# Decoding four weight blocks beside the last two pairs of k, zero passes at the head, and a later transpose

## The chip, the cores and the metric

The kernel runs on one core of a Trainium2 chip. The metric is the device time of one execution in microseconds (us), here the median of three runs. The engines have short names in what follows: PE (TensorE, with PEld for its weight loads), DVE (VectorE), ACT (ScalarE), POOL (GpSimd) and SP (SyncE, which issues the DMAs here).

## The reference, cut to what matters

Linear attention with random features on `q`, `k` and `v` (2 batches, 8 heads, 576 tokens, 64 wide, 128 features), then a feed-forward layer with `h - tanh(h)`, then a sum over four experts with ReLU. The change touches the first two.

```python
def phi(x):
    proj = np.einsum('bhsd,md->bhsm', x, omega)
    h = proj - np.sum(x * x, axis=-1, keepdims=True) / 2.0
    return np.exp(h - np.max(h, axis=-1, keepdims=True)) / np.sqrt(m)
kv = np.einsum('bhsm,bhsd->bhmd', phi(k_s), v)
z = np.sum(phi(k_s), axis=2)
out = einsum(phi(q_s), kv) / (einsum(phi(q_s), z) + 1e-6)
...
h = x @ w_in          # 1152x512 by 512x2048
g = h - np.tanh(h)
y = g @ w_out
```

`w_in` and `w_out` arrive as 64-bit floats and are turned into fp32 on the chip.

## The kernel before, in words

Every product in the part at hand is made of three passes of PE on operands split into a high and a low half (`th` and `tl`, `hh` and `hl`, `wah` and `wal`): high by high, high by low, low by high.

**The k stage** (up to about 43 us). The eight heads go as four pairs `p`. A pair's tokens are nine blocks of 128 rows in five groups (`kgroups`): four groups of two blocks from `kn`, and one of the last 64 tokens of each batch from `kr`, which holds all pairs. `features` (L296) gives two lists of generators. `transposed` (L304) turns four blocks at a time on PE (L299), copies the high half (`th`, ACT L304, or DVE L302 for the second four) and makes the low half (`tl`, DVE L306). `projected` (L318) makes six matmuls into `psP` (L317; three for the last group), the negated row maxima `nm` on DVE (L320), and four exponentials `kf` on ACT (L325; two for the last group). There are two `psP` banks. The products of a pair with v (`k_products`, `psV`, L337) run beside the next pair's groups, as `post`. The loop that begins at `for p in range(NP)` writes the order of PE, DVE and ACT by hand; POOL and SP follow a scheduler. Its `turn` says which transposes stand beside which group: those of the pair's own `kr` beside its second group (`i == 1`), the next pair's beside its fourth and fifth.

**Decoding a block** (class `Decoded`). 128x512 64-bit words are loaded into `raw`, of which there are four buffers. `scaled` makes `y` on ACT (L115). `joins` makes `m` on DVE: a shift (`top`, L128, or on ACT as `topped`, L121), a join with `y` and a join with `raw` (both L131), called here shift, y and raw. `parted` splits `m`: high half on ACT (L71), low half on POOL (L72). Before the change blocks 0 and 1 of the first four of w_in (`first[0]`, `first[1]`) are decoded beside the third and the fourth pair, one step a group; blocks 2 and 3, and the four of w_out, are decoded in the q loop (`LATER`).

**The q loop** (`for u in range(1, NU + 3)`, then `for e in ...`) is ordered by a scheduler. Twelve units of q go through projection, transposes (`psQ`, `qt`), attention (`psN`, L371 and L374, divided on DVE, L376 to L378) and the way back (`psX`, `x`, L385 and L72). Behind them `early` computes the first four columns of blocks of the feed-forward layer, in twelve units of 512, 384 and 256 tokens: `pse` (L485) in a PSUM bank, then `minus_tanh`, whose steps are named by letters: on ACT u (L495), q (L496), t (L497), m (L498), h (L503), on DVE a (L499), b (L500), s (L501), c (L502), and l on POOL (L504). Step s overwrites `pse` with `pse - t`, and c copies that into `y` where a mask says so, so the bank is held until c.

**Behind it** (from `po`, L598, at 125 us) the feed-forward layer runs in an order written by hand, then the experts. Lines of the profile are those of the kernel before.

Of the kernel before, what the change touches and what calls it, by code (L numbers as in the profile page):

```python
# [26 lines left out]
def tile_favor_attention__then__two_moe(  # L27
# [231 lines left out]
    load_v(1)  # L259
    ob = [ac.tile([P, 2 * P], F32R, name=f"ob{a}") for a in range(2)]  # L260
# [151 lines left out]
    LATER = {j - 1: (load_a, wa, 0, j) for j in range(2, NJ)} | {3 + j: (load_b, wb, 0, j) for j in range(NJ)}  # L412
# [3 lines left out]
    def k_pair(p):  # L416
        rest = kr[:, 2 * p:2 * p + 2, :].rearrange("p h d -> p (h d)")
        kT[p], kR[p] = features(lambda b, h: kn[p][:, b, h], rest, kgroups, lambda: kf[p], kp, k=True)

    first = {}  # L420
    with tc.manual_schedule(engines={mybir.EngineType.DVE, mybir.EngineType.PE, mybir.EngineType.Activation}):
        transposed_omega()
        k_pair(0)
        for i in range(2):
            whole(kT[0][i])
        post = []
        for p in range(NP):
            w = [first[p - 2].scaled, *first[p - 2].joins()] if p > 1 else []
            kf[p] = kp.tile([P, NT, 2, M], F32, tag="xf", name="kf")
            for i in range(len(kgroups)):  # L430
                if i == 3 and p + 1 < NP:
                    k_pair(p + 1)
                turn = kT[p][2:] if i == 1 else kT[p + 1][i - 3:i - 2] if i > 2 and p + 1 < NP else []
                run(lambda x=x: next(x) for x in turn)
                R = kR[p][i]
                next(R)
                next(R)
                run(lambda x=x: next(x) for x in turn)
                next(R)
                run(post[i:i + 1])  # L440
                run(w[i:i + 1])
                if i == 1 and p + 2 < NP:
                    kn.append(load_k(p + 2))
                    first[p] = load_a(0, p)
            if p > 1:
                wa[0, p - 2] = first[p - 2].parted()
# [44 lines left out]
    def minus_tanh(ps, hh, hl, t, u, y, view, eng_lo):  # L491

        vec, act = nc.vector, nc.scalar
        return dict(
# [6 lines left out]
            s=lambda: vec.tensor_tensor(out=ps, in0=ps, in1=view(t), op=ALU.subtract),  # L501
            c=lambda: vec.copy_predicated(view(y), view(u).bitcast(I32), ps),  # L502
# [24 lines left out]
    def early(e):  # L527
# [10 lines left out]
        g = minus_tanh(ps, gs[0, j][0][:, s], gs[0, j][1][:, s], t, u, y, lambda z: z, nc.gpsimd)  # L538
# [439 lines left out]
```

## Time and profile before

| | |
|---|---|
| median of three runs | 682.95 us (681.95 to 683.59) |
| the profiled execution | 683.97 us, of which 681.8 is the span |
| busy share of the span | PE 97%, DVE 78%, ACT 47%, POOL 10% |
| chain that ended last | PE 77%, DVE 13%, ACT 6% |
| recorded clock of PE | 1.000 |

The span counts from the first instruction to the last; the 2.2 us around it belong to every run. A row of a timeline gives start and duration in us, engine, line, operation, output and inputs, and in brackets how long its engine stood idle before and what ended that. Starts of neighbours on one engine can be closer than the duration, since operations overlap at their ends. The end of a matmul is modelled, so a busy PE may hide short pauses.

### The profile page before, as it was taken

To read this page: it belongs to the slowest core of one execution; us is meant where nothing else is said; L and a number is where in the kernel's file an instruction comes from. 1 tells how busy PE (TensorE), PEld (TensorE's weight loads), DVE (VectorE), ACT (ScalarE), POOL (GpSimd) and SP (SyncE) were. 2 spreads that over 40 slices of the span, in tenths; PEclk is the share of its full clock that TensorE was granted. 3 is DMA by queue.
4 is the path that set the end of the run, shared out by engine and by line. 5 is a ranking of instruction groups with operands and counts; after the bars stand their busy time and mean duration, and the time that the engine had idled before them with its cause. 6 is when DMAs were issued, how large, how long until landed. Compare 5 with 4: busy or idle time off the path is not lost.

```text
span 681.8 us, 10488 instructions
## 1 busy us (share of the span) xinstructions
PE 664.7 (97%) x4219; PEld 615.2 (90%) x4219; DVE 532.9 (78%) x832; ACT 317.1 (47%) x589; POOL 67.5 (10%) x66
## 2 busy tenths in 40 slices
PE   5999999899999999999999999999999999999997
PEld 4879889899999999998899999999988999999996
DVE  4788789799999987969387777777776777777664
ACT  4789998767767757435122223222232223232120
POOL 2032113522222210100000000000000000000000
PEclk9999999999999999999999999999999999999999
DMA  7953110212222222012001011111212020120004
GB/s 200 290 181 93 63 32 4 91 62 75 90 84 82 87 50 92 31 38 56 1 31 62 32 32 62 42 51 32 62 32 62 32 62 32 32 62 1 1 1 139
DMA packets 42768, 43.75 MB, mean 64 GB/s; under 512 B 5600, under 2 KB 37600, under 8 KB 42720
## 3 DMA queue, kind: packets, MB, share of 16 engines
q1 hardware_dynamic: 42720, 43.08, 21.1%
q8 instruction: 33, 0.54, 0.3%
q14 instruction: 15, 0.12, 0.1%
HBM read 40.72 MB, written 2.36 MB: 63 GB/s over the span
## 4 chain that ended last, share of the span: by engine, by line
PE 77%; DVE 13%; ACT 6%; issue 2%; DMA 1%; SPq 0%; POOL 0%; DVEq 0%
PE po L719 29%; PE Y L702 23%; PE po L598 7%; PE psh L485 7%; PE psP L317 3%; DVE m L131 3%; PE pse L485 2%; DVE y L499 2%; PE psN L371 2%; DVE y L502 1%; DVE y L500 1%; ACT y L496 1%; PE psQ L360 1%; ACT m L121 1%; DVE psh L501 1%
## 5 line engine op out<-in xcount | busy, mean ns | idle before, releaser
L725 DVE SCALAR_TENSOR_TENSOR oacc<-po,pr,oacc 128x512 f32<-128x512 f32 (+1 forms) x136 | 101.4, 746 | 34.2 <-PE po L719 33.8
L719 PE MATMUL po<-wbh,hl 128*128 128x512 f32 x290 | 112.9, 389 | 0.4 <-DVE hl L522 0.4
L719 PE MATMUL po<-wbh,hh 128*128 128x512 f32 x290 | 112.9, 389 | 0.1
L719 PE MATMUL po<-wbl,hh 128*128 128x512 f32 x290 | 112.9, 389 | 0.0
L719 PEld LDWEIGHTS po<-wbh,hl 128*128 128x128 f32 x290 | 54.4, 188 | 12.3 <-DVE hl L522 0.8
L719 PEld LDWEIGHTS po<-wbh,hh 128*128 128x128 f32 x290 | 54.7, 188 | 8.2 <-DVE oacc L725 0.3
L598 PE MATMUL po<-hh,wbh 128*128 128x384 f32 x180 | 60.8, 338 | 0.7 <-DVE y L502 0.5
L719 PEld LDWEIGHTS po<-wbl,hh 128*128 128x128 f32 x290 | 54.4, 188 | 7.5
L890 ACT ACTIVATE hh<-Y 128x576 fp32r<-128x576 f32 x42 | 27.4, 653 | 72.5 <-DVE Y L887 64.0
L598 PE MATMUL po<-hl,wbh 128*128 128x384 f32 x180 | 60.7, 337 | 0.2
L598 PE MATMUL po<-hh,wbl 128*128 128x384 f32 x180 | 60.4, 336 | 0.0
L702 PE MATMUL Y<-y,wah 128*128 128x288 f32 x336 | 57.9, 294 | 0.0
L485 PE MATMUL psh<-x,wah 128*128 128x384 f32 x288 | 57.9, 336 | 0.0
L702 PEld LDWEIGHTS Y<-y,wah 128*128 128x128 f32 x336 | 51.2, 188 | 3.6 <-DVE hl L522 0.3
L485 PEld LDWEIGHTS psh<-x,wah 128*128 128x128 f32 x288 | 50.5, 188 | 0.0
L702 PE MATMUL Y<-Th,wal 128*128 128x288 f32 x224 | 47.8, 295 | 0.0
L702 PE MATMUL Y<-Tl,wah 128*128 128x288 f32 x224 | 47.6, 294 | 0.0
L702 PE MATMUL Y<-Th,wah 128*128 128x288 f32 x224 | 47.6, 293 | 0.0
L890 ACT ACTIVATE hh<-u 128x576 fp32r<-128x576 f32 x14 | 9.6, 687 | 73.5 <-DVE u L887 73.5
L702 PEld LDWEIGHTS Y<-Th,wah 128*128 128x128 f32 x224 | 39.0, 188 | 4.5
L503 ACT ACTIVATE hh<-y 128x1152 fp32r<-128x1152 f32 (+3 forms) x26 | 20.7, 798 | 41.7 <-DVE y L502 41.7
L672 ACT ACTIVATE wah<-y 128x512 fp32r<-128x512 f32 x28 | 17.6, 631 | 41.1 <-DVE y L652 41.1
(140 smaller groups left out, 1464.5 us busy)
## 6 DMA issues: line engine op xcount, KB each, us to landing
raw<-in_moe_w_dram SPq DMA_DIRECT2D x30, 512.0 KB, 3.6
raw<-in_moe_w_in_dram SPq DMA_DIRECT2D x16, 512.0 KB, 3.6
raw<-in_moe_w_out_dram SPq DMA_DIRECT2D x16, 512.0 KB, 3.4
kn<-in_k_dram SPq DMA_DIRECT2D x8, 256.0 KB, 4.4
vn<-in_v_dram SPq DMA_DIRECT2D x8, 256.0 KB, 5.6
qn<-in_q_dram SPq DMA_DIRECT2D x8, 256.0 KB, 5.4
out_dram<-oacc SPq DMA_DIRECT2D x7, 256.0 KB, 2.2
raw<-in_moe_w_dram SPq DMA_DIRECT2D x4, 256.0 KB, 2.9
```

The source lines that it names most:

```text
L131: vec.scalar_tensor_tensor(out=self.m, in0=x, scalar=scalar, in1=self.m, op0=op, op1=ALU.bitwise_or)
L317: nc.tensor.matmul(ps[:, i].rearrange("p a m -> p (a m)"), x[:, c], o, start=j == 0, stop=j == 2)
L371: nc.tensor.matmul(ps[:, j, h, :VC], qt[g][:, j, h, :], kvz[p][:, t // (TB + 1), h, :], start=True, stop=True)
L485: nc.tensor.matmul(ph[i, j][:, n, :CH] if bank is None else bank, w[:, c], x[:, n * CH:(n + 1) * CH] if bank is None else x[:, n], start=z ...
L499: a=lambda: vec.scalar_tensor_tensor(out=y, in0=y, scalar=CB, in1=u, op0=ALU.add, op1=ALU.mult),
L503: h=lambda: act.activation(hh, y, AF.Copy),
L598: nc.tensor.matmul(po[:, :CH], w[:, r], g[:, s], start=j == 0 and z == 0, stop=j == NJ - 1 and z == 2,)
L672: nc.scalar.activation(w[0], src, AF.Copy)
L702: nc.tensor.matmul(ps[:, m, :HN // 2], w[:, kk], b[:, m * HN // 2:(m + 1) * HN // 2], start=first and kk == 0 and z == 0, stop=kk == 1 and ...
L719: nc.tensor.matmul(po, g[:, s], w[:, cols], start=j == 0 and z == 0, stop=j == 1 and z == 2)
L725: nc.vector.scalar_tensor_tensor(out=acc, in0=po, scalar=pr[:, t, e:e + 1], in1=acc, op0=ALU.mult, op1=ALU.add)
L890: nc.scalar.activation(halves(gs[NA + q, f][0][:, h * HN:(h + 1) * HN]), x, AF.Relu)
```

## The change

Four things. Before the k stage PE makes matmuls over a tile of zeros into a spare `psN` bank: six ahead of the transpose of omega, six behind it, two between the first two sets of four transposes. For the first pair, the transpose of its `kr` tokens moves from the second group to the fourth, and that of the next pair's first half from the fourth to the third. Blocks 0 and 1 of w_in are decoded beside the third pair, 2 and 3 beside the fourth, the second of each two one group behind the first; the blocks of w_out move up by one unit of the q loop. And in `early` step s writes its difference to `t` in SBUF, and c reads it there.

```diff
+    zero = kp.tile([P, 2 * P], F32R, name="zero", bufs=1)
+    nc.vector.memset(zero.bitcast(F32), 0.0)
+    idle = ps_n.tile([P, 512], F32, tag="n", name="idle")
+    def busy(n):
+        for _ in range(n):
+            nc.tensor.matmul(idle[:, :2 * P], zero[:, :P], zero, start=True, stop=True)
...
-    LATER = {j - 1: (load_a, wa, 0, j) for j in range(2, NJ)} | {3 + j: (load_b, wb, 0, j) for j in range(NJ)}
+    LATER = {2 + j: (load_b, wb, 0, j) for j in range(NJ)}
...
+    def turns(p, i):
+        if i == 1 + 2 * (p == 0):
+            return kT[p][2:]
+        if p + 1 < NP and i in ((2, 4) if p == 0 else (3, 4)):
+            return kT[p + 1][i == 4:1 + (i == 4)]
+        return []
...
+        busy(6)
         transposed_omega()
+        busy(6)
         k_pair(0)
         for i in range(2):
             whole(kT[0][i])
+            if i == 0:
+                busy(2)
         post = []
         for p in range(NP):
-            w = [first[p - 2].scaled, *first[p - 2].joins()] if p > 1 else []
+            w = [[first[j].scaled, *first[j].joins()] for j in range(2 * p - 4, 2 * p - 2)] if p > 1 else []
             kf[p] = kp.tile([P, NT, 2, M], F32, tag="xf", name="kf")
             for i in range(len(kgroups)):
-                if i == 3 and p + 1 < NP:
+                if i == 2 and p + 1 < NP:
                     k_pair(p + 1)
-                turn = kT[p][2:] if i == 1 else kT[p + 1][i - 3:i - 2] if i > 2 and p + 1 < NP else []
+                turn = turns(p, i)
...
-                run(w[i:i + 1])
+                for z, x in enumerate(w):
+                    if i >= z:
+                        run(x[i - z:i - z + 1])
                 if i == 1 and p + 2 < NP:
                     kn.append(load_k(p + 2))
-                    first[p] = load_a(0, p)
+                if i == 1 and p < 3 or (p, i) == (1, 3):
+                    first[len(first)] = load_a(0, len(first))
             if p > 1:
-                wa[0, p - 2] = first[p - 2].parted()
+                for j in range(2 * p - 4, 2 * p - 2):
+                    wa[0, j] = first[j].parted()
...
+        d = view(t) if free else ps
...
-            s=lambda: vec.tensor_tensor(out=ps, in0=ps, in1=view(t), op=ALU.subtract),
-            c=lambda: vec.copy_predicated(view(y), view(u).bitcast(I32), ps),
+            s=lambda: vec.tensor_tensor(out=d, in0=ps, in1=view(t), op=ALU.subtract),
+            c=lambda: vec.copy_predicated(view(y), view(u).bitcast(I32), d),
...
-        g = minus_tanh(ps, gs[0, j][0][:, s], gs[0, j][1][:, s], t, u, y, lambda z: z, nc.gpsimd)
+        g = minus_tanh(ps, gs[0, j][0][:, s], gs[0, j][1][:, s], t, u, y, lambda z: z, nc.gpsimd, free=True)
```

How the order of instructions moves, at three places. Lines of the changed kernel are 9 to 27 higher. The first is ACT in the first pair of k, from the first `th`; before:

```order
L304 ACTIVATE th_153<-psT_155 128x512
L325 ACTIVATE kf_169<-psP_170,nm_177 128x128 x4
L304 ACTIVATE th_153<-psT_183 128x128
L325 ACTIVATE kf_169<-psP_186,nm_193 128x128 x4
L325 ACTIVATE kf_169<-psP_205,nm_212 128x128 x4
L304 ACTIVATE th_218<-psT_220 128x512
L325 ACTIVATE kf_169<-psP_226,nm_233 128x128 x4
L325 ACTIVATE kf_169<-psP_246,nm_250 128x128 x2
```

and now:

```order
L313 ACTIVATE th_168<-psT_170 128x512
L334 ACTIVATE kf_186<-psP_187,nm_194 128x128 x4
L334 ACTIVATE kf_186<-psP_200,nm_207 128x128 x4
L313 ACTIVATE th_218<-psT_220 128x512
L334 ACTIVATE kf_186<-psP_226,nm_233 128x128 x4
L313 ACTIVATE th_168<-psT_240 128x128
L334 ACTIVATE kf_186<-psP_243,nm_250 128x128 x4
L334 ACTIVATE kf_186<-psP_263,nm_267 128x128 x2
```

The `th` of the `kr` tokens (128x128) stood behind the first four exponentials and stands behind the third four; the next pair's first `th` (tile `th_218`) is now ahead of it.

The second is DVE from the last `kvz` copy inside the fourth pair to the residuals `tl` of q; before:

```order
L342 COPY kvz2_141<-psV_543 128x260
L131 SCALAR_TENSOR_TENSOR m_597<-raw_310,m_597 128x512
L320 TENSOR_REDUCE nm_652<-psP_648 128x2
L131 SCALAR_TENSOR_TENSOR m_825<-y_823,m_825 128x512
L128 TENSOR_SCALAR m_906<-raw_902 128x512
L131 SCALAR_TENSOR_TENSOR m_825<-raw_821,m_825 128x512
L131 SCALAR_TENSOR_TENSOR m_906<-y_904,m_906 128x512
L306 TENSOR_TENSOR tl_663<-psT_665,th_662 128x512
```

and now (`sm` and `pr` are the sums over the experts' shares, which stood at the end of the q loop):

```order
L351 COPY kvz2_144<-psV_574 128x260
L131 SCALAR_TENSOR_TENSOR m_628<-raw_393,m_628 128x512
L131 SCALAR_TENSOR_TENSOR m_656<-y_630,m_656 128x512
L329 TENSOR_REDUCE nm_688<-psP_684 128x2
L131 SCALAR_TENSOR_TENSOR m_656<-raw_479,m_656 128x512
L128 TENSOR_SCALAR m_935<-raw_931 128x512
L598 TENSOR_REDUCE sm_1922<-pr_72 128x9
L131 SCALAR_TENSOR_TENSOR m_935<-y_933,m_935 128x512
L599 TENSOR_SCALAR sm_1922<-sm_1922 128x9
L131 SCALAR_TENSOR_TENSOR m_935<-raw_931,m_935 128x512
L128 TENSOR_SCALAR m_1022<-raw_1018 128x512
L315 TENSOR_TENSOR tl_704<-psT_706,th_703 128x512
```

Behind the last maximum of k (128x2) there were a y, a shift, a raw and a y join ahead of `tl`; now there are three joins, two shifts and two operations on `sm`, and between the copy and that maximum one join more.

The third is DVE at the end of the q loop, from a raw join that both have there; before:

```order
L131 SCALAR_TENSOR_TENSOR m<-raw,m 128x512
L500 SCALAR_TENSOR_TENSOR y<-y,pse 128x384
L501 TENSOR_TENSOR pse<-pse,t 128x384
L572 TENSOR_SCALAR sm<-sm 128x9
L131 SCALAR_TENSOR_TENSOR m<-y,m 128x512
L502 COPY_PREDICATED y<-u,pse 128x384
L499 SCALAR_TENSOR_TENSOR y<-y,u 128x256
L573 RECIPROCAL sm<-sm 128x9
L500 SCALAR_TENSOR_TENSOR y<-y,pse 128x256
L501 TENSOR_TENSOR pse<-pse,t 128x256
L574 TENSOR_TENSOR pr<-pr,sm 128x36
L131 SCALAR_TENSOR_TENSOR m<-raw,m 128x512
```

and now:

```order
L131 SCALAR_TENSOR_TENSOR m<-raw,m 128x512
L527 SCALAR_TENSOR_TENSOR y<-y,pse 128x384
L528 TENSOR_TENSOR t<-pse,t 128x384
L72 TENSOR_TENSOR x_806<-psX,x_805 128x256
L529 COPY_PREDICATED y<-u,t 128x384
L526 SCALAR_TENSOR_TENSOR y<-y,u 128x384
L527 SCALAR_TENSOR_TENSOR y<-y,pse 128x384
L528 TENSOR_TENSOR t<-pse,t 128x384
L529 COPY_PREDICATED y<-u,t 128x384
```

A y and a raw join and the operations on `sm` and `pr` are gone from between the steps of `early`; steps s and c, now L528 and L529, name `t` in place of `pse`.

## Rows read from the trace of the kernel before

**Rows 1.** Stretches: us, then PE, PEld, DVE, ACT, POOL busy; clock, DMA share, GB/s.

```profile
35.10:43.00 7.90, 7.27 (x119) 6.38 (x118) 6.11 (x13) 7.36 (x25) 1.87 (x2) 1.00 0.49 146
...
50.00:103.00 53.00, 52.65 (x411) 47.76 (x410) 45.40 (x117) 48.97 (x128) 10.25 (x8) 1.00 0.20 63
103.00:125.20 22.20, 19.66 (x134) 18.41 (x132) 21.21 (x49) 19.44 (x49) 10.97 (x9) 1.00 0.13 41
```

**Rows 2.** Timeline of PE, end of q loop: start, us, operation, [idle <-releaser].

```profile
116.39 0.39 PE L485 MATMUL pse<-x,wah 128*128 128x256 f32 x1 [0.71 <-DVE x L72]
...
123.03 0.51 PE L485 MATMUL pse<-x,wah 128*128 128x256 f32 x2 [1.36 <-DVE y L502]
...
125.17 0.44 PE L598 MATMUL po<-hh,wbh 128*128 128x384 f32 x1 [0.47 <-DVE y L502]
```

**Rows 3.** Timeline of the head, PE and ACT.

```profile
4.47 1.12 PE L299 MATMUL psT<-ident,kn 128*128 128x128 f32 x4 [1.27 <-DMA kn<-in_k_dram]
...
8.98 1.14 ACT L325 ACTIVATE kf<-psP,nm 128x128 f32<-128x128 f32 x4 [2.76 <-DVE nm L320]
...
10.07 0.45 PE L299 MATMUL psT<-ident,kr 128*128 128x128 f32 x1 [1.86 <-DMA kr<-in_k_dram]
...
12.57 2.42 ACT L325 ACTIVATE kf<-psP,nm 128x128 f32<-128x128 f32 x8 [1.73 <-DVE nm L320]
...
17.17 0.63 ACT L325 ACTIVATE kf<-psP,nm 128x128 f32<-128x128 f32 x2 [0.53 <-DVE nm L320]
```

**Rows 4.** Timeline of DVE in the third pair of k.

```profile
31.31 0.69 DVE L320 TENSOR_REDUCE nm<-psP 128x4 f32<-128x512 f32 x1 [0.72 <-PE psP L317]
...
34.05 0.41 DVE L320 TENSOR_REDUCE nm<-psP 128x2 f32<-128x256 f32 x1
```

**Rows 5.** Timeline of ACT in the second to fourth pair.

```profile
25.61 0.63 ACT L325 ACTIVATE kf<-psP,nm 128x128 f32<-128x128 f32 x2 [0.72 <-DVE nm L320]
...
34.49 0.63 ACT L325 ACTIVATE kf<-psP,nm 128x128 f32<-128x128 f32 x2 [1.32 <-DVE nm L320]
...
38.50 0.73 ACT L115 ACTIVATE y<-raw 128x512 f32<-128x512 f32 x1
...
42.30 0.63 ACT L325 ACTIVATE kf<-psP,nm 128x128 f32<-128x128 f32 x2 [0.43 <-DVE nm L320]
```

**Rows 6.** Timeline from the fourth pair of k into q.

```profile
42.18 0.68 DVE L131 SCALAR_TENSOR_TENSOR m<-y,m 128x512 int32<-128x512 int32 x1
...
42.77 0.42 DVE L128 TENSOR_SCALAR m<-raw 128x512 int32<-128x512 int32 x1
...
43.52 3.11 POOL L72 TENSOR_TENSOR wal<-m,wah 128x512 fp32r<-128x512 f32 x2 [6.45 <-ACT wah L71]
43.72 1.77 DVE L131 SCALAR_TENSOR_TENSOR m<-y,m 128x512 int32<-128x512 int32 x1
...
45.41 1.27 DVE L306 TENSOR_TENSOR tl<-psT,th 128x512 fp32r<-128x512 f32 x2
```

**Rows 7.** Timeline of PE, single matmuls of the first pair.

```profile
10.75 0.41 PE L317 MATMUL psP<-ob,tl 128*128 128x256 f32 x1
...
14.11 0.28 PE L317 MATMUL psP<-ob,tl 128*128 128x256 f32 x1
```

**Rows 8.** DVE by form from 102 to 126 us, then two rows of its timeline.

```profile
L131 DVE SCALAR_TENSOR_TENSOR m<-y,m 128x512 int32<-128x512 int32 x2 | 2.2, 1114 | 0.0
...
113.52 1.55 DVE L131 SCALAR_TENSOR_TENSOR m<-y,m 128x512 int32<-128x512 int32 x1
...
121.19 0.42 DVE L501 TENSOR_TENSOR pse<-pse,t 128x256 f32<-128x256 f32 x1
```

**Rows 9.** DVE by form from 40 to 130 us: count, busy us, mean ns.

```profile
L499 DVE SCALAR_TENSOR_TENSOR y<-y,u 128x384 f32<-128x384 f32 x4 | 2.9, 722 | 0.3 <-ACT y L496 0.3
...
L502 DVE COPY_PREDICATED y<-u,pse 128x384 f32<-128x384 int32 x4 | 2.3, 584 | 0.0
...
L500 DVE SCALAR_TENSOR_TENSOR y<-y,pse 128x384 f32<-128x384 f32 x4 | 2.2, 545 | 0.0
```

More of the change, by code (lines that the diff above doesn't have):

```diff
@@ L489, in hidden, with minus_tanh @@
                     )
-    def minus_tanh(ps, hh, hl, t, u, y, view, eng_lo):
+    def minus_tanh(ps, hh, hl, t, u, y, view, eng_lo, free=False):
         vec, act = nc.vector, nc.scalar
+        d = view(t) if free else ps
         return dict(
```

## Prediction

> **What bounds the kernel now.** Read first the span in stretches [rows 1]: between 50 and 103 us TensorE (PE) is busy 52.65 of 53.00 us, but between 103 and 125.2 it misses 2.54. The change edits only code up to there, and what follows is the same list of instructions. So the question is how much earlier the first output product, `po` at 125.17, can start. PE's three last pauses before it [rows 2] are 0.71 us for `x` of DVE, 1.36 us for a PSUM bank that `copy_predicated` (L502) still read, and 0.47 us for the same kind of release; DVE is busy 21.21 of 22.20 us there [rows 1].
>
> At the head look at the waits in brackets [rows 3]. The second group's projection stands behind the transpose of `kr`, which waits 1.86 us for its DMA; so ACT, done with the first four exponentials at 8.98 + 1.14 = 10.12, gets the next only at 12.57.
>
> In the third pair of k look at DVE: from 31.31 on each operation starts behind the one before without a pause [rows 4], and ACT waits 1.32 us for the maximum made at 34.05 [rows 4, 5]. In the fourth, ACT is busy 7.36 of 7.90 us [rows 1], and then DVE decodes weights until it comes to the residuals `tl` of q at 45.41 [rows 6]. Both engines are full where the change adds to them.
>
> **The change, part by part.** The sum is made against the profiled execution: 681.8 us of span and 2.2 around it, 683.97. The median shown is 682.95, 1.0 lower; the difference found is carried over to it.
>
> *1. Last tokens of the first pair later.* The second group's projection now follows the first's, near 8.2 us, and its maximum is there by 10.1, so ACT goes on at about 10.15 in place of 12.57: 2.4 us earlier. From there ACT has eight exponentials (2.3), `th` of the next pair (0.6), `th` of the last tokens (0.3) and two exponentials (0.6), with one wait of some 0.5, estimated, for the last group's way through PE and DVE: that is as much as it needed between 12.57 and 17.17 + 0.63 = 17.80 with its waits, 5.2, less 0.9. `kr` had landed at 10.07 and is now wanted near 11; the second pair's `kn`, wanted near 9, was issued ahead of it on the same queue. Because later waits may come back I take the 2.4 alone: -2.4. Ends: -1.86 (the wait for `kr`) and -3.3 (those 0.9 too).
>
> *2. Passes over zeros.* Fourteen matmuls of 256 columns and a memset. The recorded clock is 1.00 throughout, the upper level of 2.4 GHz, yet such a matmul shows 0.41 us at 10.75 and 0.28 at 14.11 [rows 7]: the rows quicken only after PE had worked on from 10.07. Cost: the first six stand where PE has no operand yet; the next six take some 6 x 0.21, estimated as the start to start of the slow ones, and lie beside the wait of 1.27 for `kn` at 4.47 [rows 3]; two stand ahead of the next four transposes. With that cover the cost is 0; without it a batch of two costs 0.4. Worth: 0.13 on each of some twelve early matmuls, of which most is hidden, since the first maximum stands behind DVE's `tl`. I take 0; the ends, -0.5 and +0.4, lie inside those of part 1.
>
> *3. Third pair.* It decodes two blocks instead of one. DVE gets 0.42 for the shift (L128) and two joins (L131), 0.59 each from start to start [rows 6]. Both joins fall into the closed row from 31.31: one ahead of the last group's maximum, one ahead of the fourth pair's first. ACT gets one more scale (L115, 0.73 at 38.50, [rows 5]) behind the second group, of which about 0.2 reaches that row. So 2 x 0.59 + 0.2: +1.4. Ends: +0.44, since this pair with its one decode ends 8.88 us after the second (25.61 to 34.49), and that one with none 8.44 after the first (17.17 to 25.61) [rows 3, 5]; and +2.3, all that DVE and ACT get.
>
> *4. Fourth pair.* Again one more block, but two scales of later blocks already stood here: ACT gets one L115 more (0.73), DVE one join ahead of the last maximum (0.59). They run side by side: +0.7, ends 0 and +1.4.
>
> *5. Into q.* Between the last maximum and `tl` DVE had y, shift, raw, y: 45.41 - 42.18 = 3.2 us, of which one L131 took 1.77 while GpSimd (POOL) split two blocks [rows 6]. Now three joins, two shifts and two small sums of `pr` stand there: 3 x 0.59 + 2 x 0.42 + some 0.2 = 2.8, and with one such stretch (1.77 - 0.68 = 1.1) 3.9. Behind `tl` one join is gone, 0.6. So 0.7 - 0.6, and I take +0.3, since ACT has two splits before `th` of q now and had one; ends -0.6 and +1.2. The sums wait for the four small loads of `pr`, which on SP now stand behind a second block of w_out; that block's buffer is free some 9 us before the sums are due: 0, in the upper end.
>
> So q starts at -2.4 + 1.4 + 0.7 + 0.3 = 0.0: the head's gain is spent on decode, and behind it DVE and ACT have two blocks less to do.
>
> *6. Between 50 and 103.* PE has 0.35 us of visible idle time [rows 1]: -0.3, ends 0 and, by pauses that its modelled ends may hide, -1.2.
>
> *7. End of the q loop.* Here DVE had two y joins of 2.2 us together (one of 1.55 at 113.52), two raw joins of 0.68, one shift of 0.42 and four small steps on `pr` [rows 6, 8]: 4.0 without the small ones. One join of each kind, 1.4, stays: 2.6 less. And with the difference written to `t` in SBUF, a bank is free when L501 ends (121.19 + 0.42 = 121.61, [rows 8]), not with L502 at about 122.97, so the pause of 1.36 goes; so does that of 0.71, whose `x` stood behind the L131 of 1.55, and about half of 0.47: -2.3, ends 0 and -2.54 [rows 2]. ACT is late next: busy 19.44 of 22.20 [rows 1], it has 2.8 us to give and doesn't stop this. The new forms of L501 and L502 have no row; between L500 with PSUM data (545 ns at 384 columns) and L499 with two SBUF inputs (722, [rows 9]) they cost within 0.2 us of the old L502 (584), and I take the old.
>
> Sum: 0.0 - 0.3 - 2.3 = -2.6, so 681.4 for a profiled run and 682.95 - 2.6 = **680.3** as a median.
>
> **The rivals.**
>
> *A, the head's gain arrives.* The second decode hides as the first did: +0.44 in the third pair, +0.2 in the fourth, 0 behind. For it: one decode was nearly hidden. Against: DVE's closed row. Then q starts 1.8 us earlier, in all -4.4: 678.5.
>
> *B, ACT takes over at the end.* Without DVE's lag ACT's steps set the pace, and PE waits for them in the same places; about 1 us of part 7 is left, in all -1.0: 681.9. For it: ACT is busy 88% there. Against: it waited for DVE in that stretch.
>
> *C, slower: L502 meets GpSimd.* Now L502 reads two SBUF tiles, mask and data, as L131 and L499 do. An L131 that started 0.2 us into POOL's splits took 1.77 instead of 0.68 [rows 6], another 1.55 [rows 8], and L499 averages 722 ns where L500, with one SBUF input, averages 545 [rows 9]. Eight L502 stand in the end stretch, where POOL is busy 10.97 of 22.20 us [rows 1]. At L499's mean excess, 0.18, they cost 1.4 of the 2.6 us saved and -2.3 stands, since the banks are free before L502. From 0.33 each nothing of DVE's relief is left; if each waits as those two L131 did, 1.0, DVE ends 8.0 - 2.6 = 5.4 us later, and with 1.8 for the banks given against it the kernel is 3.6 - 0.3 = 3.3 us slower: 686.2. Against it: L499 mostly misses POOL. The Trainium skill (SBUF — State Buffer, "Who interferes with whom") has the rule that speaks against this edit: a DVE instruction with two SBUF inputs and a GpSimd instruction that reads SBUF exclude each other, and the one that starts second is blocked for the whole of the first. By that rule the trace agrees, with 1.77 us against 0.68.
>
> *D, it doesn't do what it says.* `kr`, the second `kn` or `pr` is late, and the wait only changes its place: about 2 us of the gain go, -0.6: 682.3.
>
> **How the numbers follow.** Forecast 0.50, A 0.20, B 0.14, C 0.11, D 0.05. A measurement can tell about 0.2%, 1.4 us, from no change: faster is below 681.6, slower above 684.3. The forecast has a spread of its own of some 1.5 us: 0.42 of it is faster, 0.05 the same, 0.03 slower, where parts 3 to 5 meet their upper ends (+4.9, against 2.4 taken). A is faster; of B and D 0.03 are faster and 0.16 the same; of C 0.01 is the same and 0.10 slower. Faster 0.65, same 0.22, slower 0.13. The range reaches past A's side on the one hand and to the upper ends of parts 3 to 5 on the other, without C: 677.7 to 683.6.
>
> **What would show it.** Right: no PE wait for `kr`; the first pair's last exponentials end near 15.4; the fourth pair's start within 1 us of 42.30; `tl` of q near 45.4; the first `po` near 122.6; no PE wait over 0.5 us for `copy_predicated`. Wrong: `tl` of q before 44 (A); PE waits for ACT behind 105 us (B); a mean of `copy_predicated` at 384 columns over 0.9 us (C); the first `po` behind 125.2.

## The result and the profile after

| | before | changed |
|---|---|---|
| median, 6 runs each | 683.41 us (681.95 to 685.87) | 687.61 us (686.69 to 688.64) |
| ratio | | 1.0051, 95% interval [1.0033, 1.0069] |
| profiled execution, span | 681.8 us | 685.9 us |
| recorded clock of PE | 1.000 | 0.993 |

The change makes the kernel 0.5% slower (the quotient of the two medians is 1.006); the forecast was 680.3, with a range of 677.7 to 683.6. Around the span of the changed kernel's profiled execution, 687.67 us in all, lie 1.8 us, not 2.2. In the code after, lines have moved: L299 to L308, L306 to L315, L317 to L326, L320 to L329, L325 to L334, L337 to L346, L485 to L510, L499 through L502 to L526 through L529, L598 (`po`) to L625.

The stretches of the changed kernel, columns as in [rows 1]:

```profile
35.10:43.00 7.90, 5.31 (x68) 4.72 (x68) 3.43 (x6) 4.53 (x14) 3.70 (x4) 0.78 0.66 188
43.00:50.00 7.00, 4.59 (x83) 3.93 (x79) 6.94 (x13) 5.51 (x13) 3.42 (x3) 1.00 0.53 154
50.00:70.00 20.00, 18.67 (x139) 18.41 (x139) 15.60 (x41) 15.14 (x46) 2.42 (x2) 0.83 0.26 79
70.00:103.00 33.00, 33.00 (x256) 29.31 (x255) 29.00 (x75) 30.90 (x77) 6.42 (x5) 1.00 0.16 49
103.00:125.20 22.20, 21.75 (x151) 20.87 (x150) 20.99 (x45) 19.11 (x47) 6.76 (x6) 1.00 0.15 48
```

In the fourth pair (35.1 to 43) all three engines fall together: PE 5.31 for 7.27, DVE 3.43 for 6.11, ACT 4.53 for 7.36 [rows 1]. That all go idle at once points to an operand that none of them makes. And the clock column shows 0.78, then 0.83 between 50 and 70, where it had been 1.00.

The timeline of the changed kernel at the head and around the fourth pair (SP's rows are the issues of loads, columns as in [rows 2]):

```profile
8.81 2.17 ACT L334 ACTIVATE kf<-psP,nm 128x128 f32<-128x128 f32 x8 [2.73 <-DVE nm L329]
...
14.32 0.63 ACT L334 ACTIVATE kf<-psP,nm 128x128 f32<-128x128 f32 x2 [0.26 <-DVE nm L329]
...
29.51 0.47 SPq L107 DMA_DIRECT2D raw<-in_moe_w_in_dram  x1
30.08 0.45 SPq L210 DMA_DIRECT2D vn<-in_v_dram  x1
...
31.50 0.56 SPq L210 DMA_DIRECT2D vn<-in_v_dram  x1
...
37.02 0.61 POOL L248 COPY vs<-vn 128x512 f32<-128x512 f32 x1 [13.43 <-DMA vn<-in_v_dram]
37.97 0.62 POOL L248 COPY vs<-vn 128x512 f32<-128x512 f32 x1 [0.34 <-DMA vn<-in_v_dram]
...
37.69 0.45 PE L346 MATMUL psV<-vs,kf 128*64 128x65 f32 x8 [2.72 <-POOL vs L248]
38.07 0.79 PE L326 MATMUL psP<-ob,th 128*128 128x256 f32 x2
38.66 0.41 PE L326 MATMUL psP<-ob,tl 128*128 128x256 f32 x1
...
41.72 0.29 PE L326 MATMUL psP<-ob,tl 128*128 128x256 f32 x1
...
40.48 1.14 ACT L334 ACTIVATE kf<-psP,nm 128x128 f32<-128x128 f32 x4 [2.66 <-DVE nm L329]
...
45.37 0.61 ACT L334 ACTIVATE kf<-psP,nm 128x128 f32<-128x128 f32 x2
...
46.58 3.15 POOL L72 TENSOR_TENSOR wal<-m,wah 128x512 fp32r<-128x512 f32 x2 [5.51 <-ACT wah L71]
46.74 1.25 DVE L599 TENSOR_SCALAR sm<-sm 128x9 f32<-128x9 f32 x1
...
48.51 1.50 DVE L128 TENSOR_SCALAR m<-raw 128x512 int32<-128x512 int32 x1
49.93 1.27 DVE L315 TENSOR_TENSOR tl<-psT,th 128x512 fp32r<-128x512 f32 x2
50.66 0.38 PE L326 MATMUL psP<-ob,tl 128*128 128x256 f32 x1 [1.76 <-DVE tl L315]
```

The same two loads of v and POOL's copies in the kernel before, which no row group shows:

```profile
28.50 0.37 SPq L210 DMA_DIRECT2D vn<-in_v_dram  x1
...
29.92 0.55 SPq L210 DMA_DIRECT2D vn<-in_v_dram  x1
30.52 1.39 SPq L107 DMA_DIRECT2D raw<-in_moe_w_in_dram  x1
...
32.70 0.60 SPq L107 DMA_DIRECT2D raw<-in_moe_w_in_dram  x1
...
34.34 0.62 POOL L248 COPY vs<-vn 128x512 f32<-128x512 f32 x1 [8.23 <-PE psP L317]
35.20 0.62 POOL L248 COPY vs<-vn 128x512 f32<-128x512 f32 x1 [0.24 <-DMA vn<-in_v_dram]
```

Read downward: the head's gain is there (the first pair's last exponentials start at 14.32, before at 17.17 [rows 3]). But the fourth block of w_in, 512 KB, is now issued at 29.51, ahead of the last pair's v; before, both remaining blocks stood behind it. The queue has no slack there: between 30 and 37 us the DMA share is 1.00, at 317 GB/s, so that the block's 512 KB take about 1.65 us, an estimate from that rate. v's first half is copied by POOL at 37.02 in place of 34.34 (where POOL waited for PE's release and v may have landed sooner), while the pair that wants it runs some 2 us earlier. PE has products with this v in its order ahead of projections that need none of it, and stands 2.72 us. Then its rows are slow, 0.41 us for a single matmul that shows 0.29 at 41.72. The clock of 0.83 between 50 and 70 is another stretch: it is at 0.50 from 52 to 58, behind the 1.76 us for which PE waits for `tl` at 50.66.

The way from mark to mark, in us, for the kernels that the argument uses (start of each pair's last exponentials, of the first `tl` of q, of the fourth tanh of `early`, of the first `po`; the spans are those of the profiled executions):

| | before | changed | block4_behind_v | head_v_first | decode_priced |
|---|---|---|---|---|---|
| second pair | 25.61 | 23.04 | 22.95 | 22.81 | 23.53 |
| third pair | 34.49 | 32.52 | 32.42 | 32.14 | 33.00 |
| fourth pair | 42.30 | 45.37 | 42.11 | 39.93 | 41.90 |
| `tl` of q | 45.41 | 49.93 | 46.68 | 43.04 | 46.47 |
| fourth tanh | 99.89 | 105.78 | 100.26 | 97.55 | 102.33 |
| first `po` | 125.17 | 129.23 | 123.67 | 123.19 | 125.13 |
| span | 681.8 | 685.9 | 680.3 | 679.9 | 681.8 |

From the differences of neighbours, changed less before: head -2.6, third pair +0.6, fourth pair +5.0, way into q +1.5, loop up to the fourth tanh +1.4, its end -1.8; sum +4.1, which is what the span grew by.

### The profile page after: what moved, and what is told of

The parts are those of the page before. It is cut to its first block, busy times and chain, and to the rows that moved or that the text cites. A ratio compares the mean times of both kernels' runs of the same rounds, so it can differ in the third digit from the quotient of the medians.

```text
span 685.9 us, 10514 instructions
## 1 busy us (share of the span) xinstructions
PE 669.0 (98%) x4233; PEld 620.8 (91%) x4233; DVE 537.4 (78%) x833; ACT 317.4 (46%) x589; POOL 67.2 (10%) x66
## 4 chain that ended last, share of the span: by engine, by line
PE 77%; DVE 12%; ACT 6%; DMA 2%; issue 2%; SPq 0%; POOL 0%; DVEq 0%; POOLq 0%
PE po L746 29%; PE Y L729 23%; PE po L625 7%; PE psh L510 7%; PE psP L326 3%; PE pse L510 2%; DVE m L131 2%; PE psN L380 2%; DVE y L526 2%; DVE y L527 1%; DVE y L529 1%; PE psQ L369 1%; ACT y L523 1%; DVE psh L528 1%; ACT m L121 1%
## 5 line engine op out<-in xcount | busy, mean ns | idle before, releaser
L625 PE MATMUL po<-hl,wbh 128*128 128x384 f32 x180 | 60.7, 337 | 0.4 <-DVE hl L531 0.3
L625 PE MATMUL po<-hh,wbh 128*128 128x384 f32 x180 | 60.7, 337 | 0.3
L625 PE MATMUL po<-hh,wbl 128*128 128x384 f32 x180 | 60.4, 336 | 0.0
L510 PE MATMUL psh<-x,wah 128*128 128x384 f32 x288 | 57.7, 336 | 0.0
L510 PEld LDWEIGHTS psh<-x,wah 128*128 128x128 f32 x288 | 50.5, 188 | 0.0
L329 DVE TENSOR_REDUCE nm<-psP 128x4 f32<-128x512 f32 (+1 forms) x40 | 25.2, 633 | 15.3 <-PE psP L326 14.9
```

The lines of the kernel that those rows point to most:

```text
L329: nc.vector.tensor_reduce(out=nm[:, :n], in_=ps[:, :n], op=ALU.max, axis=AX.X, negate=True)
L510: nc.tensor.matmul(ph[i, j][:, n, :CH] if bank is None else bank, w[:, c], x[:, n * CH:(n + 1) * CH] if bank is None else x[:, n], start=z ...
L625: nc.tensor.matmul(po[:, :CH], w[:, r], g[:, s], start=j == 0 and z == 0, stop=j == NJ - 1 and z == 2,)
```

## The experiments

Two theories. **Late v**: the load of the fourth block makes the last pair's v late, and PE's pause for it, with the clock that follows, is the loss. **Decode work**: the joins, shifts and scales added to full engines are the loss. Each time is compared with runs of the kernel before on the same chip; a ratio below 1 is faster than that kernel, and its 95% interval stands behind it.

**Only the order of loads (two kernels).** In both, the orders of PE, DVE, ACT and POOL stay as in the changed kernel.

```diff
@@ qloads_behind_v, in place of the eight loads at p == 1
+            for p2 in {1: range(1), 2: range(1, NP)}.get(p, ()):
+                for b in range(B):
+                    load_full(q, b, p2, qn[:, b, 2 * p2:2 * p2 + 2])
@@ block4_behind_v
-                if i == 1 and p < 3 or (p, i) == (1, 3):
+                if i == 1 and p < 2 or i == 3 and p in (1, 2):
```

> The changed kernel with one thing moved: six of the eight loads of q (the second to fourth pair's) are issued behind the last pair's v; the orders of PE, DVE, ACT and POOL stay word for word. Theory (late v): the last pair's v was the late operand: issued at 30.08 and 31.50, copied by POOL at 37.02 and 37.97, with PE waiting 2.72 us for it and then granted 0.78 of its clock. Here v is issued near 24.5 and 26 and copied by 32; PE's wait for POOL's copy goes, the stretch 35.1 to 43 is at clock 1.00, the fourth pair's last exponentials begin near 41.5 to 42.5 in place of 45.37, and the time is 3 to 5 us below the changed kernel: 682.6 to 684.6. Rival (the decode work itself, on DVE and ACT in the third and fourth pair and into q): nothing is taken off those engines, so the wait only turns into one for DVE or ACT, and the time stays within 1 us of 687.6. Third possibility: the loads of q are late in their turn and PE waits for qn near 46.

> The changed kernel with one thing moved: the load of the fourth block of w_in (512 KB) is issued behind the last pair's v, not ahead of it. Theory (late v): v is issued some 1.5 us earlier, as before the change (28.5 and 29.9), and PE's wait of 2.72 us for POOL's copy shrinks to about 1.2; the time falls by 1 to 3 us, to 684.6 to 686.6, unless the block itself, which is wanted by ACT's scale in the fourth pair's second group, is then late and ACT waits for it (then the gain is smaller and ACT shows a wait for raw). Rival (decode work): within 1 us of 687.6.

Measured: qloads_behind_v 682.78 us against 684.21 (ratio 0.998 [0.9969, 0.9992]), block4_behind_v 683.61 (0.9992 [0.9977, 1.0008]). Each takes 4 us or more off the changed kernel by moving loads alone, block4_behind_v more than the 1 to 3 us expected. In block4_behind_v, stretches and timeline:

```profile
35.10:43.00 7.90, 5.92 (x95) 5.14 (x97) 6.81 (x14) 7.07 (x22) 3.30 (x3) 1.00 0.56 171
```

```profile
34.34 0.61 POOL L248 COPY vs<-vn 128x512 f32<-128x512 f32 x1 [12.64 <-DMA vn<-in_v_dram]
...
42.11 0.62 ACT L334 ACTIVATE kf<-psP,nm 128x128 f32<-128x128 f32 x2
...
45.26 1.50 DVE L128 TENSOR_SCALAR m<-raw 128x512 int32<-128x512 int32 x1
46.68 1.27 DVE L315 TENSOR_TENSOR tl<-psT,th 128x512 fp32r<-128x512 f32 x2
```

In this execution no wait for POOL's copy is left on PE, DVE is busy 6.81 us again, the clock is 1.00, and the fourth pair ends 3.3 us earlier than in the changed kernel. So late v, with what follows from it, is worth 4.0 to 4.8 us of the medians, as much as the change lost against the kernel before. The order of loads doesn't remove the wait in every execution: splits_behind_q, no_zeros and zeros_in_pause (below) have it too, and their profiled executions show v's copy at 35.08, 35.92 and 36.64 and PE waits for it of 0.69, 1.50 and 1.97 us. The third block's load, in the changed kernel also ahead of v, at 17.47, isn't to blame: with neither block ahead (no_second_block, below) v is copied at 34.98, no earlier than here. Two details of the expectations for qloads_behind_v fell: v was issued at 28.48, not near 24.5, since the queue still held other loads, and a block of w_out then came late, so that ACT waited 1.21 us for it and the pair ended at 43.20. And neither kernel reaches the forecast: a second loss remains.

**Products behind the pair.** The step into q is taken into the hand-written order.

```diff
-    interleave([lambda: q_emit(0, "R", 0), lambda: q_emit(1, "T", 0), lambda: q_emit(0, "R", 1)], post)
+        interleave([lambda: q_emit(0, "R", 0), lambda: q_emit(1, "T", 0), lambda: q_emit(0, "R", 1)], post)
```

> The changed kernel, with its loads as they are (v late), but the step into q written in hand order too, so that the products of the last pair with v stand behind that pair's projections on PE, not among them. Theory: v's lateness costs only because products with it stand in PE's order ahead of projections that have their operands; here PE doesn't wait for POOL's copy inside the fourth pair, whose last exponentials start near 42 to 43 in place of 45.37, and the time falls by 2 to 4 us (683.6 to 685.6), part of which the changed order into q may take back. Rival (v's lateness isn't what holds the pair): last exponentials still behind 44.5.

688.57 us (1.0079 [1.0058, 1.0099]): a miss. PE no longer waits for POOL's copy, as expected, but the last exponentials start at 43.90, between what the theory (42 to 43) and its rival (behind 44.5) said. DVE's and POOL's timelines of this run:

```profile
39.68 1.48 DVE L128 TENSOR_SCALAR m<-raw 128x512 int32<-128x512 int32 x1 [1.18 <-POOL wal L72]
...
36.51 1.45 POOL L248 COPY vs<-vn 128x512 f32<-128x512 f32 x2 [13.26 <-PE psP L326]
37.92 2.94 POOL L72 TENSOR_TENSOR wal<-m,wah 128x512 fp32r<-128x512 f32 x2
```

v's lateness has a second way in: POOL copies v first and splits two blocks behind it, DVE's shift wants the `m` buffer that those splits release, and the next maximum stands behind that shift. So PE's order was not the only thing that held the pair. The new order into q also left PE waiting 3.69 us for `kf` and 2.30 for `tl`; the time says nothing of v alone.

**Parts taken back one by one.** no_second_block is the changed kernel with the old decode and loads of w_in; no_free has the subtraction in PSUM again; free_alone is the kernel before with the subtraction into `t`; block4_no_free is block4_behind_v with no_free's edit; no_zeros is that without the fourteen passes and their memset.

```diff
@@ no_second_block
-    LATER = {2 + j: (load_b, wb, 0, j) for j in range(NJ)}
+    LATER = {j - 1: (load_a, wa, 0, j) for j in range(2, NJ)} | {3 + j: (load_b, wb, 0, j) for j in range(NJ)}
...
-            w = [[first[j].scaled, *first[j].joins()] for j in range(2 * p - 4, 2 * p - 2)] if p > 1 else []
+            w = [first[p - 2].scaled, *first[p - 2].joins()] if p > 1 else []
...
@@ no_free, block4_no_free
-        g = minus_tanh(ps, gs[0, j][0][:, s], gs[0, j][1][:, s], t, u, y, lambda z: z, nc.gpsimd, free=True)
+        g = minus_tanh(ps, gs[0, j][0][:, s], gs[0, j][1][:, s], t, u, y, lambda z: z, nc.gpsimd)
@@ no_zeros
-        busy(6)
         transposed_omega()
-        busy(6)
...
-            if i == 0:
-                busy(2)
```

> The changed kernel with the decode as it was (one block of w_in in each of the third and fourth pair, two inside the loop over q, the loads of w_in as before), but with the earlier head, the zeros and the subtraction into t. Theory (late v): v is issued near 28.5 again, while the pairs run some 2.5 us earlier; so PE waits about 1 us for POOL's copy, q starts some 1.5 to 2.5 us earlier than before the change, and the end of the loop gives about 1 us: 679.5 to 682. Rival (decode work is the whole loss): the head's full 2.85 us arrives at q: 678.5 to 680. If neither is so and the head or the subtraction itself costs, the time is above 683.4.

> The changed kernel with the subtraction written into PSUM as before (L528 and L529 on the bank), all else as changed. It prices the subtraction into t in this schedule: the forecast put about 1.8 us of the end's gain on the bank's release. Expected: 1 to 2 us slower than the changed kernel (688.6 to 689.6), with PE waits of 1 us and more for the select at the end of the loop; if the select with two SBUF inputs costs more than the release gives (rival C of the prediction), it is faster than 687.6.

> The changed kernel with the fourth block's load behind the last pair's v, and the subtraction written back into PSUM as before. It prices the subtraction into t without the disturbance that v's lateness brings. From the way between the fourth early tanh and the first output product: 25.28 us in the kernel before, 23.45 in the changed one, 22.77 without the subtraction into t. So theory (the select with two SBUF inputs costs more than the bank's release gives): 0.7 us faster than the same kernel with it: 682.9. Rival, as the forecast had it (the release gives 1.8 us): 685.4.

> The kernel before with the subtraction into t alone. Theory (select with two SBUF inputs against POOL): 0 to 1 us slower than before, most likely +0.7, with the select's mean at 256 columns near 0.8 us in place of 0.44. Rival, the forecast's part 7 (the bank is free sooner and PE's pause of 1.36 us goes): 1 to 2 us faster.

> As block4_no_free, without the fourteen passes over zeros and their memset. The forecast valued them at 0, with ends -0.5 and +0.4: so within 0.5 us of block4_no_free. If they keep the early rows quick (0.28 in place of 0.41 us for a single matmul from 7.5 us on), the first pair ends later here by up to 0.5 us; if they stand in the way, earlier.

Measured: no_second_block 683.46 (0.9994 [0.9978, 1.0011]), no_free 686.6 (1.0043 [1.0024, 1.0063]), block4_no_free 683.61 (0.9999 [0.9984, 1.0015]), free_alone 684.17 against 683.62 (1.0013 [0.9997, 1.0028]), no_zeros 683.47 (1.0004 [0.9989, 1.0018]).

*The subtraction into `t`* gives nothing. In free_alone the subtraction is L502 and the select (`copy_predicated`) L503. Its PE pauses at the end of the loop, its stretch, and the select by form:

```profile
122.83 0.51 PE L485 MATMUL pse<-x,wah 128*128 128x256 f32 x2 [2.00 <-DVE t L502]
...
125.56 0.44 PE L599 MATMUL po<-hh,wbh 128*128 128x384 f32 x1 [1.05 <-DVE t L502]
```

```profile
103.00:125.20 22.20, 19.51 (x137) 18.70 (x135) 22.00 (x48) 18.29 (x45) 12.36 (x10) 1.00 0.15 48
```

```profile
L503 DVE COPY_PREDICATED y<-u,t 128x384 f32<-128x384 int32 x4 | 3.2, 811 | 0.0
...
L503 DVE COPY_PREDICATED y<-u,t 128x256 f32<-128x256 int32 x3 | 2.4, 804 | 0.2
```

The select of 256 columns in the kernel before, from 103 to 128 us:

```profile
L502 DVE COPY_PREDICATED y<-u,pse 128x256 f32<-128x256 int32 x3 | 1.3, 441 | 0.2
```

The bank is now freed by the subtraction, but PE waits 2.00 and 1.05 us where it waited 1.36 and 0.47 [rows 2]: the select costs 811 ns for 584 [rows 9] at 384 columns and 804 for 441 at 256, DVE is busy 22.00 of 22.20 us, and being later it frees the bank no sooner. These means hide two kinds: at 384 columns three selects take 0.60 or 0.61 us and one, which starts at 119.18 inside a POOL split (118.60 to 120.15), takes 1.43; at 256 two take 0.45 and 0.65, and one, which starts at 123.09 as a POOL split does (123.08), takes 1.32. That is rival C's mechanism nearly at its price, some 0.85 us for each select that meets POOL where it said 1.0, but two of these seven paid it in full, not all. The Trainium skill's rule that it cited (SBUF — State Buffer, "Who interferes with whom") is borne out by these rows. From the fourth tanh to `po` it is 25.15 us here and 25.28 before; with the second decode out of the loop 23.41 (block4_behind_v) and 22.78 without the subtraction into `t` (block4_no_free). The medians of the last two are equal, and decode_priced (below), which is qloads_behind_v without this edit, stands at 0.9988 to its 0.998; so in time it is worth nothing measurable either way.

*no_free* was expected 1 to 2 us slower than the changed kernel and came out 1.0 faster, which the two intervals don't tell from nothing. Its profiled execution is the slowest of its eight (690.06): the loads are ordered as in the changed kernel, but v was copied at 38.97, PE waited 4.47 us, and the clock in 35.1 to 43 was 0.62. So the lateness itself varies from run to run.

*no_second_block* missed its 679.5 to 682. PE waits 1.05 us for POOL's copy, as expected, so the earlier head by itself makes v late; `tl` is 1.1 us earlier than before, not 1.5 to 2.5; and that is given back at the end, where DVE, with the old decode and the dearer select, made PE wait 1.99 and 1.05.

*The zeros* are worth nothing, as forecast: no_zeros and block4_no_free differ by 0.14 us.

**The way into q, and the clock.** splits_behind_q is block4_no_free with two splits emitted behind q's first transposes; zeros_in_pause adds twelve passes over zeros there; head_splits moves the last pair's one split in the same way in the kernel head_v_first (below).

```diff
@@ splits_behind_q
-            if p > 1:
-                for j in range(2 * p - 4, 2 * p - 2):
+            if p == 2:
+                for j in range(2):
                     wa[0, j] = first[j].parted()
...
         q_emit(0, "T", 0)
+        for j in range(2, NJ):
+            wa[0, j] = first[j].parted()
@@ zeros_in_pause, ahead of those two lines
+        idle = ps_e.tile([P, 512], F32, tag="e", name="idle")
+        fill[0] = idle
+        busy(12)
```

> As block4_no_free, and the splits of the third and fourth block of w_in (ACT's copy, POOL's remainder) are emitted behind q's first two transposes, not ahead of them. Theory for the way into q: two small DVE operations (L599 at 1.25 us, L128 at 1.50) each waited out a POOL split there, and tl came at 46.68 where the kernel with the old decode has it at 44.33; with the splits behind, tl is near 44.3 to 45, and the time 1.5 to 2.3 us lower than block4_no_free: 680.6 to 681.5. Rival (DVE's added joins and shifts alone set it): tl stays above 46 and the time within 0.5 us.

> As splits_behind_q, with twelve passes over zeros between q's first transposes, in the pause of 1.85 us in which PE there waits for the last exponentials of k (41.4 to 43.27), after which its rows were slow (granted clock 0.76 between 43 and 50). Nothing else is moved. Theory (PE's pauses cost twice, once as waiting and once through the clock granted behind them): the rows from 44 to 47 stay quick, the stretch 43 to 50 is at 1.00, and the time is 1 to 2 us below splits_behind_q (681.5 to 682.5). Rival (the slow rows lie beside other work and cost nothing, or the clock falls for another reason): within 0.5 us of 683.5.

> As head_v_first, with the last pair's split of a block of w_in emitted behind q's first transposes. There a join took 1.77 us beside POOL's two splits (41.35) ahead of tl. Expected: the join at 0.7, tl near 42 in place of 43.04, and 0.5 to 1 us less: 681.1 to 681.6. Rival (POOL's splits then meet the next operations of DVE, as in splits_behind_q, where the second tl came no earlier): within 0.5 us of 682.1.

Measured: splits_behind_q 683.49 (0.9998 [0.998, 1.0017]), zeros_in_pause 683.04 against 683.96 (1.0 [0.9984, 1.0017]), and head_splits 683.37 against 683.71 (0.9998 [0.9987, 1.001]). In splits_behind_q the first `tl` did come at 44.24, as expected, but the second only at 46.31, behind a join that met POOL's splits in its turn (1.54 us), and the clock fell. Stretches from 44 to 48 and two rows of PE, splits_behind_q:

```profile
44.00:46.00 2.00, 2.00 (x29) 1.71 (x25) 2.00 (x3) 2.00 (x4) 1.44 (x2) 0.53 0.80 227
46.00:48.00 2.00, 2.00 (x15) 1.88 (x12) 1.22 (x3) 0.68 (x2) 2.00 (x2) 0.61 0.62 174
...
43.27 0.91 PE L346 MATMUL psV<-vs,kf 128*64 128x65 f32 x22 [1.85 <-ACT kf L334]
...
48.24 0.80 PE L346 MATMUL psV<-vs,kf 128*64 128x65 f32 x20
```

The same with zeros_in_pause:

```profile
44.00:46.00 2.00, 2.00 (x34) 1.58 (x34) 1.99 (x5) 2.00 (x6) 0.14 (x1) 1.00 0.87 265
46.00:48.00 2.00, 2.00 (x32) 1.87 (x30) 2.00 (x3) 1.63 (x4) 2.00 (x2) 1.00 0.90 205
...
44.58 0.91 PE L346 MATMUL psV<-vs,kf 128*64 128x65 f32 x22
...
48.07 0.80 PE L346 MATMUL psV<-vs,kf 128*64 128x65 f32 x20
```

With the pause filled the clock stays at the upper level. The passes themselves end before these stretches begin, and in this execution v was 1.6 us later than in the other (36.64 against 35.08), so the same products stand 1.3 us later in them; counted from row to row, the way between these two groups of products takes 3.49 us with the pause filled and 4.97 without. So in this pair of executions the pause ahead of these rows, not the work in them, goes with the lower clock. In time nothing is shown: the median is 0.45 us lower, where 1 to 2 were expected, but by the ratios to the kernel before the two are equal. head_splits brought the first `tl` to 42.76 and no gain: the collision with POOL moves on to the next operation, as its rival said. Its time is 1.1 us above head_v_first by the ratios, outside the rival's 0.5; why, no run shows.

**The faster version, and the decode's price.**

head_v_first is the kernel before with the change's head and zeros and the edit of qloads_behind_v; decode_priced adds the change's decode and its loads. Against the changed kernel, head_v_first takes back the decode as no_second_block does and the subtraction as no_free does:

```diff
-        g = minus_tanh(ps, gs[0, j][0][:, s], gs[0, j][1][:, s], t, u, y, lambda z: z, nc.gpsimd, free=True)
+        g = minus_tanh(ps, gs[0, j][0][:, s], gs[0, j][1][:, s], t, u, y, lambda z: z, nc.gpsimd)
...
-    LATER = {2 + j: (load_b, wb, 0, j) for j in range(NJ)}
+    LATER = {j - 1: (load_a, wa, 0, j) for j in range(2, NJ)} | {3 + j: (load_b, wb, 0, j) for j in range(NJ)}
...
+            for p2 in {1: range(1), 2: range(1, NP)}.get(p, ()):
```

> The kernel before with the earlier head and the zeros alone (decode and subtraction as before), and the loads of q's second to fourth pair behind the last pair's v. Theory (the head's gain is real, and what ate it was v's lateness and then the decode): PE has no wait for POOL's copy of v, the fourth pair ends 2.2 to 2.85 us earlier than before (39.5 to 40.1), tl of q stands near 42.8, nothing is given back at the end, and the time is 680.5 to 682. Rival (an earlier q is given back inside the loop over q or at its end): tl early, but the first output product still near 125 and the time above 683.

> head_v_first with the changed kernel's decode (two blocks in each of the third and fourth pair, the loads for it as in the change) and nothing else: it prices the move of the decode alone, with v as early as it can be had beside the fourth block's load. The forecast: +2.4 us up to q and -2.6 behind, about 0. From the traces so far: third pair +0.6, fourth +1.7, way into q +1.5, so q 3.7 us later, and 2.5 less at the end: +1.2 us, 683.3. If v or the blocks are late in the fourth pair, or PE's pauses there pull its clock down, more: up to 685.

head_v_first: 682.11 us against 683.96, ratio 0.9982 [0.9968, 0.9996]; faster than the kernel before, and by that and 1.0051 some 0.7% faster than the changed one. Its POOL and DVE rows:

```profile
29.20 0.61 POOL L248 COPY vs<-vn 128x512 f32<-128x512 f32 x1 [4.93 <-PE psV L346]
...
43.04 1.28 DVE L315 TENSOR_TENSOR tl<-psT,th 128x512 fp32r<-128x512 f32 x2
```

In this execution v's copy is 5 us earlier than before, `tl` of q 2.4 us, and `po` 2.0 us: most of the head's gain arrives once v doesn't hold it. By the ratio it is 1.2 us in the time. decode_priced: 682.91 against 683.71 (0.9988 [0.9977, 0.9999]), which the times can't tell from head_v_first. Their profiled executions can (table above): from the second pair to `tl` of q decode_priced takes 22.94 us for 20.23, from there to the fourth tanh 55.86 for 54.51 with the clock at 0.79 between 43 and 50 and 0.90 between 50 and 70, and then 22.80 for 25.64. So in these executions the moved decode costs 2.7 and 1.4 us and gives back 2.8, where the forecast had 2.4 against 2.6. They are unequal executions, head_v_first's at a clock of 1.00 throughout, decode_priced's the slowest of its eleven, and the 1.4 is the clock's: with the moved decode and the clock at 1.00 between 50 and 70 the way from `tl` to the fourth tanh takes 53.58 us (block4_behind_v and qloads_behind_v alike), 0.9 less than in head_v_first. The lower clock stands behind PE waits of 1.27 and 1.76 us on the way into q (42.32 and 47.20); it comes without late v too, here and in block4_no_free (0.88 between 43 and 50).

## Why the prediction was wrong, point by point

- **Part 1, the gain: right.** Forecast -2.4, found -2.85 at the first pair and -2.57 at the second. **Part 1, the check of what is wanted earlier: the step that failed.** It looked at `kr` and the second `kn`, part 5 at `pr`; it did not look at the last pair's v, which this earlier loop wants 2 us sooner, and which the fourth block's load, that part 4 counted only as a scale and a join, pushes back on SP's queue by 1.6 us at issue and 2.7 at POOL's copy. PE waited 2.72 us for it, and part 4's +0.7 became +5.0, of which 3.2 went when that load was moved. Moving loads alone took 4.0 (block4_behind_v) and 4.8 us (qloads_behind_v) off the time. Rival D named a late load as the case, but named three others and -0.6 for it.
- **Part 2: right**, 0.
- **Part 3: over-sized.** +1.4 forecast, +0.6 found: nearly the lower end, one more decode hid as the first had.
- **Part 4: under-sized.** +0.7 forecast; with v in time the fourth pair takes 42.11 - 32.42 = 9.69 us for 7.81, +1.9, beyond the upper end of 1.4. The two scales that "already stood here" still stand; with one more, a shift (0.95 us at 36.39 in block4_behind_v) and joins met POOL's copies and splits.
- **Part 5: under-sized.** +0.3 forecast, +1.4 to +1.5 found, above the upper end. It allowed one collision with POOL; there were two, and they struck small operations: a sum of 0.17 us took 1.25, a shift of 0.42 took 1.50.
- **Part 6** assumed a clock of 1.00, and where that holds it is within its ends: -0.3 forecast, -0.9 from `tl` to the fourth tanh in block4_behind_v. In the changed kernel the clock is 0.83 between 50 and 70, and the same way takes 1.4 us longer than before. The forecast had no term for slow rows behind PE's pauses.
- **Part 7: about the right size, by the wrong half.** -2.3 forecast, -1.8 found. Forecast were 2.6 us of relief for DVE and some 1.8 from the earlier bank; the relief came (-2.5 without the subtraction into `t`), the bank's gain did not.
- **The rivals.** A's `tl` before 44 and B's wait for ACT did not come; C's collisions came nearly at their price, but for a few selects (two of seven in free_alone; in the changed kernel one of four at 384 columns took 0.95 us for 0.59); none was the case that happened, since none had a load that the change itself put ahead of another. Of the signs of being wrong, `po` behind 125.2 came (129.23).
- **The sums.** Three don't close, and none decides the outcome: B leaves out part 6's -0.3 (with it -1.3, 681.7); the upper ends of parts 3 to 5 alone make 682.8, not the 683.6 of the range nor a time called slower; and C's eight `copy_predicated` in the end stretch are seven in the trace of the kernel before.

## What to carry to other kernels

When a change makes a loop earlier, list every operand that the loop reads, and for each the place of its load on the queue before and after; a load added for other work counts as work on the path of all that stand behind it. A load whose user comes late (the six loads of q here) can be moved back, so reorder the queue before adding to it, but look at what then stands behind it: in qloads_behind_v a block of w_out came 1.21 us late. And a pause of PE can have two prices, the wait and slow rows behind it; where it can't be removed, cheap passes in it may keep the clock up, but see whether the time follows; here it didn't measurably.

## What the hardware did that was not expected

- PE's clock fell to the lower level (1.2 GHz) behind pauses of 1.76 to 4.47 us between the fourth pair and the q loop: 0.50 from 52 to 58 behind 1.76 (changed kernel), stretches at 0.53 and 0.61 behind 1.85 (splits_behind_q), 0.78 behind 2.72 (changed kernel), 0.62 behind 4.47 (no_free); but pauses of 1.86 and 1.76 in block4_behind_v left it at 1.00. Matmuls that took 0.28 us then take 0.41. The Trainium skill (TensorE: Matmul & The Clock Gate, "What's actually happening") says that the clock follows how busy PE has lately been; the filled pause, at 1.00, agrees.
- The times go along with it: of the 35 runs of the kernel before beside free_alone, the 26 with a mean clock of at least 0.999 average 683.4 us, the 7 at 0.997 or less 684.4. At 0.997 or less were 10 of the 12 runs of block4_behind_v, whose profiled execution at 1.00 is its fastest, and 10 of the 11 of decode_priced. In splits_behind_q it was 6 of 12 and with the pause filled (zeros_in_pause) 1 of 12, on another chip.
- A DVE operation on nine columns took 1.25 us beside POOL's split and 0.17 alone (43.82 in qloads_behind_v). It ended at 47.99, as the split did that had begun at 46.58 (1.39 us, to 47.97): here the cost of meeting POOL was POOL's remaining time, not a share of one's own.
